# A 32-step V sum written as a register loop on TensorE, with the engine's program laid on a boundary

## The chip, the cores and the metric

The kernel runs on one NeuronCore of one Trainium2 chip. The core has five engines with an instruction stream each: TensorE (PE, matrix products; PEld is its weight loads), VectorE (DVE), ScalarE (ACT), GpSimd (POOL) and SyncE (SP), which here issues the large transfers. Sixteen DMA engines move data between HBM and the core's memories. The metric is the device time of one execution in microseconds, and the lower the better.

## The reference

One decode step of a transformer block: a single token `x` of 1024 values goes through a layernorm, and then through two branches in parallel, whose sum is added to `x`.

```python
q = (xn @ wq).reshape(1, 1, 32, 128)                 # 32 heads of 128
k, v = the last 4096 positions of 4 kv heads          # each serves 8 heads
o = softmax(q k^T / sqrt(128)) v                      # per head
a = o.reshape(1, 1, 4096) @ wo
h = gelu(layernorm(xn) @ w1 + b1)                     # 3584 hidden values
b = h @ w2 + b2
out = x + a + b      # x's own part enters with b2 in the first accumulation
```

All inputs are bf16. K, V and the four weight matrices are 39.85 MB in all, and each byte is read once.

## The kernel before, in words

**Slots and transfers.** The large operands go through a ring of four slots of 32 KB per partition (`slots`, line 64). Slot 0 holds k_sb, then w11, then wo0; slot 1 wq0, w10, w21; slot 2 wq1, v_sb, wo1; slot 3 the transposed K's scratch kt_scr, then w20. SP issues them in this order: K (four DMAs, line 74), wq0 and wq1 (line 91), w10 and w11 (line 203), V (three DMAs, line 209), w20 and w21 (line 217), wo0 in one DMA and wo1 in five (line 225), and the output last (line 354). A transfer into a slot waits, on SP, for the last reader of what the slot held. For wo1 that is the V sum, the matmuls that read v_sb. Every DMA adds to one of eight counters (semaphores) at its landing; the Tile framework hands them out in turn and writes all waits. K's fourth DMA counts on the eighth of them, and the next that counts there is w20.

**The attention.** K is transposed in blocks of 32 by VectorE (line 187), and the blocks are set in order by ScalarE and VectorE (lines 194 and 197) while TensorE makes q from wq (line 234). Scores for 4096 positions and 32 heads stand as four bands of 32 partitions with 1024 columns (line 272). Maximum, exponential (line 294) and a block transpose (line 296) give `eTb`, a tile of 128 partitions by 1024, in which columns 32c to 32c+31 are the 32 heads' weights for the 128 positions of chunk c. The V sum (lines 314 to 317) adds up over the 32 chunks c: weights `eTb[:, 32c:32c+32]`, moving data 512 columns of V (four kv heads of 128), result `o_all` of 32 heads by 512. A mask picks each head's own kv head, VectorE divides by the softmax sum and reduces (lines 319 to 323), and four small matmuls and a copy (lines 326 and 328) turn the result into `o8`, one column per step for Wo.

**The MLP.** w1's products (line 254) stand on TensorE between the steps of the softmax; gelu (line 309) and a transpose (line 311) give `hT`.

**The output.** w2 in 28 steps and Wo in 32 are taken as one list, `chunk_src`. All but the last eight steps add into `accf`, two halves of 512 columns (line 335); the last eight into `acct`, four quarters of 256 (line 350). When accf is done, four copies, by VectorE and ScalarE in turn, bring it into `bulk` (lines 345 and 347). VectorE adds acct and bulk into `res` (line 353), and SP writes it out. On TensorE the order is the one just told: V sum, o8, w20's steps, w21's, wo0's, wo1's. TensorE's stream is in order.

Of the kernel before, what the change touches and what calls it, by code (L numbers as in the profile page):

```python
# [8 lines left out]
FP32 = mybir.dt.float32  # L9
BF16 = mybir.dt.bfloat16  # L10
ACT = mybir.ActivationFunctionType
ALU = mybir.AluOpType
# [4 lines left out]
def kernel(  # L17
# [14 lines left out]
    nc = tc.nc  # L32
    P = 128
    D = A_x.shape[-1]
    Hkv = A_k_cache.shape[1]
    Sk = A_k_cache.shape[2]
    Dh = A_k_cache.shape[3]
    NQ = A_wq.shape[1]
    Hq = NQ // Dh
# [4 lines left out]
    NCH = W // P  # L44
    NJQ = NQ // 512
    WQ4 = W // 4
# [8 lines left out]
    consts = ctx.enter_context(tc.tile_pool(name="consts", bufs=1))  # L55
# [4 lines left out]
    ps_f = ctx.enter_context(tc.tile_pool(name="ps_f", bufs=2, space=bass.MemoryType.PSUM))  # L60
# [6 lines left out]
        return ring.tile([P, RING_ELEMS], BF16, tag=f"ring{slots[name]}", name=name, align_bytes=256)  # L67

    x_flat = A_x.rearrange("a b d -> (a b d)")


    k_sb = ring_tile("k_sb")
# [103 lines left out]
    for half in range(2):  # L176
        pr = 32 * half
        nc.tensor.matmul(accf[pr:pr + 1, :], lhsT=ones_bf[pr:pr + 2, 0:1], rhs=xb2[pr:pr + 2, :],
                         start=True, stop=False, tile_position=(pr, pr))
# [12 lines left out]
    for s in range(NS):  # L192
        for (R, Cd) in pairs[:ACT_PAIRS]:
            nc.scalar.copy(out=kT[32 * Cd:32 * Cd + 32, R, s, :].rearrange("p (c j) -> p c j", j=32),  # L194
                           in_=T5[32 * R:32 * R + 32, s, :, Cd, :])
    for (R, Cd) in pairs[ACT_PAIRS:]:
        nc.vector.tensor_copy(out=kT[32 * Cd:32 * Cd + 32, R, :, :].rearrange("p s (c j) -> p (s c) j", j=32),  # L197
                              in_=kt_scr[32 * R:32 * R + 32, :].rearrange("p (c a j) -> p c a j", a=4, j=32)[:, :, Cd, :])
# [7 lines left out]
    v4 = v_sb[:].rearrange("p (g c d) -> p g c d", g=Hkv, c=NCH)  # L206
# [22 lines left out]
    for i, w3 in enumerate(wq_tiles):  # L229
        for r in range(4):  # L230
            c = 4 * i + r
            for j in range(NJQ):
                b, t = divmod(j, 4)
                nc.tensor.matmul(accq[32 * t:32 * t + 1, b, :], lhsT=xnT[:, c:c + 1], rhs=w3[:, r, j * 512:(j + 1) * 512],  # L234
                                 start=(c == 0), stop=(c == C - 1), tile_position=(0, 32 * t))
# [8 lines left out]
    for j in range(8):  # L244
        t, b = divmod(j, 2)
        nc.tensor.matmul(acch[32 * t:32 * t + 1, b, :NH], lhsT=ones_bf[0:1, 0:1], rhs=b1_row[:, j * NH:(j + 1) * NH],
                         start=True, stop=False, tile_position=(0, 32 * t))
    for i, w3 in enumerate(w1_tiles):
        for r in range(4):
            c = 4 * i + r  # L250
            for b in range(2):
                for t in range(4):
                    j = 2 * t + b
                    nc.tensor.matmul(acch[32 * t:32 * t + 1, b, :NH], lhsT=yT[:, c:c + 1], rhs=w3[:, r, j * NH:(j + 1) * NH],  # L254
                                     start=False, stop=(c == C - 1), tile_position=(0, 32 * t))
# [11 lines left out]
    for a in range(WQ4 // 512):  # L267
        sp = ps_f.tile([P, 512], FP32, tag="pf", name="sp")
        for R in range(4):
            for g in range(Hkv):  # L270
                kv = kT[:, R, :, :].rearrange("p u (b r h) -> p h b u r", r=8, h=Hkv)[:, g, 16 * a:16 * a + 16]
                nc.tensor.matmul(sp[32 * R:32 * R + 32, :].rearrange("p (b r u) -> p b u r", r=8, u=4), lhsT=qm[:, g, :], rhs=kv,  # L272
                                 start=(g == 0), stop=(g == Hkv - 1), tile_position=(0, 32 * R))
# [18 lines left out]
    l_loc = small.tile([P, 1], FP32, tag="l_loc")  # L292
    e128 = consts.tile([P, WQ4], BF16)
    nc.scalar.activation(out=e128[:], in_=sc[:], func=ACT.Exp, bias=nmx[:], scale=scale, accum_out=l_loc[:])  # L294
    eTb = consts.tile([P, WQ4], BF16)
    nc.vector.transpose(out=eTb[:], in_=e128[:])
    rs_ps = ps_f.tile([Hq, 1], FP32, tag="pf", name="rs_ps")
    nc.tensor.matmul(rs_ps[:], lhsT=sel4[:], rhs=l_loc[:], start=True, stop=True)
    rs = small.tile([Hq, 1], FP32, tag="rs")
# [1 line left out]
    grs = small.tile([Hq, Hkv], FP32, tag="grs")  # L301
# [9 lines left out]
    nc.vector.transpose(out=hT[:], in_=h_sb[:].rearrange("p (d c) -> p c d", c=CW2))  # L311


    o_all = ps_f.tile([Hq, Hkv, Dh], FP32, tag="pf", name="o_all")
    for c in range(NCH):
        nc.tensor.matmul(o_all[:].rearrange("h g d -> h (g d)"), lhsT=eTb[:, 32 * c:32 * c + 32], rhs=v4[:, :, c, :],  # L316
                         start=(c == 0), stop=(c == NCH - 1))
    o_m = consts.tile([Hq, Hkv, Dh], FP32)
    nc.vector.tensor_tensor(out=o_m[:], in0=o_all[:], in1=grs[:].unsqueeze(2).to_broadcast([Hq, Hkv, Dh]), op=ALU.mult)  # L319
    o_f = consts.tile([Hq, Dh], FP32)  # L320
    nc.vector.tensor_reduce(out=o_f[:], in_=o_m[:].rearrange("h g d -> h d g"), axis=AX.X, op=ALU.add)
    o_bf = consts.tile([Hq, Dh], BF16)
# [10 lines left out]
    for idx, (kind, c, wap) in enumerate(chunk_src[:n_bulk]):  # L333
        for half in range(2):
            nc.tensor.matmul(accf[32 * half:32 * half + 1, :], lhsT=vec[kind](c), rhs=wap[:, half * 512:(half + 1) * 512],  # L335
                             start=False, stop=(idx == n_bulk - 1), tile_position=(0, 32 * half))
# [11 lines left out]
    for idx, (kind, c, wap) in enumerate(chunk_src[n_bulk:]):  # L348
        for t in range(4):
            nc.tensor.matmul(acct[32 * t:32 * t + 1, :], lhsT=vec[kind](c), rhs=wap[:, t * 256:(t + 1) * 256],  # L350
                             start=(idx == 0), stop=(idx == TAIL - 1), tile_position=(0, 32 * t))
# [33 lines left out]
```

## Time and profile before

Three runs took 102.22, 102.37 and 102.55 us; the median is 102.37. The profile is of one more execution, of which it gives the span (first to last instruction) and no wall time.

| | us |
|---|---|
| median of three runs | 102.37 |
| span of the profiled execution | 100.73 |
| median less span | 1.64 |
| TensorE matmuls busy | 46.8 (46% of the span) |
| VectorE busy | 45.6 (45%) |
| ScalarE busy | 32.1 (32%) |
| GpSimd busy | 4.5 (4%) |
| DMA, queue of the large transfers | 39.85 MB, 92.8% of 16 engines' span |
| V sum, line 316 | 32 matmuls, 7.1 busy, 379 ns mean of one |

The mean duration of a matmul is longer than its share of the time, since matmuls overlap in the array: 32 of 379 ns take 7.07 us from the first's start to the last's end. In the rows, a shape such as 128x512 is partitions by elements, and 128*32 before it is the part of the array that is used, rows by columns. "DMA x<-y" is a transfer, "SPq" is SP's issuing of it, and "[1.65 <-DMA v_sb...]" is the idle time ahead of a group and what ended it. The granted clock is TensorE's, 1.00 is full speed. Registers, branches and semaphore instructions are not counted as busy time of an engine.

### The profile page before, as it was taken

How to read it: one execution, taken by the hardware profiler on the slowest of the kernel's cores; microseconds unless marked ns; L12 is line 12 of the kernel's file. 1: busy time of each engine (PE TensorE's matmuls, PEld its weight loads, DVE VectorE, ACT ScalarE, POOL GpSimd, SP SyncE). 2: the span in 40 equal slices, each digit the busy share in tenths (PEclk: the TensorE clock that was granted, in tenths of full speed). 3: DMA queues.
4: the chain of work that ended last, by engine and by line, in shares of the span. 5: the costliest groups of instructions: out<-in, count | busy, mean ns of one | idle time of the engine just before them, and what ended most of it. 6: DMA issues, size and time to landing. Idle time of an engine off the chain costs nothing.

```text
span 100.7 us, 934 instructions
## 1 busy us (share of the span) xinstructions
PE 46.8 (46%) x361; PEld 18.6 (18%) x361; DVE 45.6 (45%) x63; ACT 32.1 (32%) x35; POOL 4.5 (4%) x18
## 2 busy tenths in 40 slices
PE   0250300007500940048956357991980980299830
PEld 0120200002100300024402233431320320033310
DVE  4650369999999999941215246009000000000220
ACT  0500000899999999940020453000000000000110
POOL 7160200000000000000000000000000000000000
PEclk9999999999995579555599999999578599958995
DMA  1999999999999899898999998998999999999910
GB/s 27 393 417 417 416 429 494 442 455 455 429 416 390 376 512 387 376 524 376 381 420 426 433 525 387 447 451 376 490 410 425 416 416 429 416 420 415 393 41 1
DMA packets 2646, 39.92 MB, mean 396 GB/s; under 512 B 457, under 2 KB 465, under 8 KB 850
## 3 DMA queue, kind: packets, MB, share of 16 engines
q1 hardware_dynamic: 2488, 39.85, 92.8%
q8 instruction: 3, 0.05, 0.2%
q10 hardware_dynamic: 154, 0.01, 0.1%
q14 instruction: 1, 0.01, 0.0%
HBM read 39.86 MB, written 0.00 MB: 396 GB/s over the span
## 4 chain that ended last, share of the span: by engine, by line
DMA 82%; PE 11%; SPq 2%; issue 1%; DVE 0%; DVEq 0%
DMA wo<-in_A_wo_dram 27%; DMA wq<-in_A_wq_dram 26%; DMA v_sb<-in_A_v_cache_dram 23%; PE o_all L316 7%; DMA k_sb<-in_A_k_cache_dram 5%; PE accq L234 4%; SPq L225 2%; SPq L209 1%; DVE res L353 0%; PE acct L350 0%; DVEq L353 0%
## 5 line engine op out<-in xcount | busy, mean ns | idle before, releaser
L194 ACT COPY kT<-kt_scr 32x1024 bf16<-32x1024 bf16 x24 | 25.0, 1042 | 13.8 <-DVE kt_scr L187 13.5
L187 DVE STREAM_TRANSPOSE kt_scr<-k_sb 128x4096 bf16<-128x4096 bf16 x4 | 17.4, 4413 | 1.0 <-DMA k_sb<-in_A_k_cache_dram 1.0
L234 PE MATMUL accq<-wq,xnT 128*1 128x512 bf16 x64 | 7.0, 618 | 18.3 <-DMA wq<-in_A_wq_dram 18.3
L197 DVE COPY kT<-kt_scr 32x4096 bf16<-32x4096 bf16 x10 | 12.2, 1219 | 0.2
L345 DVE COPY bulk<-accf 1x256 f32<-1x256 f32 x2 | 0.8, 416 | 24.6 <-PE accf L335 24.1
L347 ACT COPY bulk<-accf 1x256 f32<-1x256 f32 x2 | 0.7, 362 | 34.3 <-DVE bulk L345 34.3
L335 PE MATMUL accf<-w,hT 128*1 128x512 bf16 x56 | 9.5, 514 | 2.8 <-DMA w<-in_B_w_dram 2.8
L335 PE MATMUL accf<-wo,o 128*1 128x512 bf16 x48 | 7.0, 464 | 5.0 <-DMA wo<-in_A_wo_dram 5.0
L316 PE MATMUL o_all<-v_sb,eTb 128*32 128x512 bf16 x32 | 7.1, 379 | 1.6 <-DMA v_sb<-in_A_v_cache_dram 1.6
L234 PEld LDWEIGHTS <-xnT 128*1 128x1 bf16 x64 | 2.1, 116 | 22.4 <-issue 22.4
L272 PE MATMUL sp<-kT,qm 128*32 128x512 bf16 x32 | 6.0, 949 | 0.3 <-DVE qm L263 0.3
L258 PE MATMUL qT_ps<-ident,q_sb 128*128 128x128 bf16 x8 | 1.2, 308 | 7.7 <-DVE q_sb L237 7.7
L335 PEld LDWEIGHTS <-hT 128*1 128x1 bf16 x56 | 3.0, 106 | 8.8 <-issue 7.5
L335 PEld LDWEIGHTS <-o 128*1 128x1 bf16 x48 | 2.5, 98 | 9.5 <-issue 7.6
L316 PEld LDWEIGHTS <-eTb 128*32 128x32 bf16 x32 | 3.0, 97 | 5.6 <-issue 2.1
L254 PE MATMUL acch<-w,yT 128*1 128x448 bf16 x64 | 3.4, 352 | 0.0
L272 PEld LDWEIGHTS <-qm 128*32 128x32 bf16 x32 | 2.3, 165 | 3.3 <-issue 3.3
L319 DVE TENSOR_TENSOR o_m<-o_all,grs 32x512 f32<-32x512 f32 x1 | 0.7, 679 | 4.9 <-PE o_all L316 4.9
L277 ACT COPY sc<-sp 128x512 f32<-128x512 f32 x1 | 0.6, 587 | 7.1 <-PE sp L272 7.1
L311 DVE STREAM_TRANSPOSE hT<-h_sb 128x896 bf16<-128x896 bf16 x1 | 1.7, 1719 | 2.4 <-ACT h_sb L309 2.4
L275 DVE COPY sc<-sp 128x512 f32<-128x512 f32 x1 | 0.7, 692 | 3.8 <-PE sp L272 3.8
L294 ACT ACTIVATE e<-sc,nmx 128x1024 bf16<-128x1024 f32 x1 | 1.1, 1147 | 3.9 <-DVE nmx L291 3.9
(84 smaller groups left out, 34.3 us busy)
## 6 DMA issues: line engine op xcount, KB each, us to landing
w<-in_B_w_dram SPq DMA_DIRECT2D x4, 3584.0 KB, 22.2
wq<-in_A_wq_dram SPq DMA_DIRECT2D x2, 4096.0 KB, 23.1
k_sb<-in_A_k_cache_dram SPq DMA_DIRECT2D x4, 1024.0 KB, 7.4
wo<-in_A_wo_dram SPq DMA_DIRECT2D x1, 4096.0 KB, 28.2
v_sb<-in_A_v_cache_dram SPq DMA_DIRECT2D x1, 2048.0 KB
v_sb<-in_A_v_cache_dram SPq DMA_DIRECT2D x2, 1024.0 KB, 22.5
wo<-in_A_wo_dram SPq DMA_DIRECT2D x1, 2048.0 KB
wo<-in_A_wo_dram SPq DMA_DIRECT2D x1, 1024.0 KB
```

What stands on the lines that cost most here:

```text
L187: nc.vector.transpose(out=scr[:, s, :], in_=k2[:, s, :])
L194: nc.scalar.copy(out=kT[32 * Cd:32 * Cd + 32, R, s, :].rearrange("p (c j) -> p c j", j=32), in_=T5[32 * R:32 * R + 32, s, :, Cd, :])
L197: nc.vector.tensor_copy(out=kT[32 * Cd:32 * Cd + 32, R, :, :].rearrange("p s (c j) -> p (s c) j", j=32), in_=kt_scr[32 * R:32 * R + 32, :] ...
L225: nc.sync.dma_start(out=tv[:, a:b, :], in_=wo_v[:, nr * i + a:nr * i + b, :])
L234: nc.tensor.matmul(accq[32 * t:32 * t + 1, b, :], lhsT=xnT[:, c:c + 1], rhs=w3[:, r, j * 512:(j + 1) * 512], start=(c == 0), stop=(c == C ...
L254: nc.tensor.matmul(acch[32 * t:32 * t + 1, b, :NH], lhsT=yT[:, c:c + 1], rhs=w3[:, r, j * NH:(j + 1) * NH], start=False, stop=(c == C - 1) ...
L258: nc.tensor.transpose(qT_ps[:, b * 4 + hh, :], q_sb[:, b, hh * Dh:(hh + 1) * Dh], ident[:])
L272: nc.tensor.matmul(sp[32 * R:32 * R + 32, :].rearrange("p (b r u) -> p b u r", r=8, u=4), lhsT=qm[:, g, :], rhs=kv, start=(g == 0), stop=( ...
L294: nc.scalar.activation(out=e128[:], in_=sc[:], func=ACT.Exp, bias=nmx[:], scale=scale, accum_out=l_loc[:])
L311: nc.vector.transpose(out=hT[:], in_=h_sb[:].rearrange("p (d c) -> p c d", c=CW2))
L316: nc.tensor.matmul(o_all[:].rearrange("h g d -> h (g d)"), lhsT=eTb[:, 32 * c:32 * c + 32], rhs=v4[:, :, c, :], start=(c == 0), stop=(c == ...
L335: nc.tensor.matmul(accf[32 * half:32 * half + 1, :], lhsT=vec[kind](c), rhs=wap[:, half * 512:(half + 1) * 512], start=False, stop=(idx == ...
```

## The change

Three things change.

- At the start of the body, `nc.tensor.addr_align(256, 0, 0)` makes the loader put TensorE's next instruction on a multiple of 256 instructions; TensorE branches over the padding.
- `eTb` gets 96 more columns, set to zero by GpSimd, and each step of the V sum takes 128 weight columns instead of 32: those of chunk c and of the three chunks behind it. The result tile `o_win` has 128 rows, of which the first 32 are the V sum as before, and the others are not read.
- Of the 32 steps, the first two and the last two stand alone, and the 28 between are a loop of 14 rounds on TensorE with two steps in a round. The addresses of weights and moving data come from registers. A round has, besides two weight loads and two matmuls, three packed register instructions (of six, two and six operations), two single ones and a compare-and-branch.

The whole stands in a critical section. In the built program, every engine's stream is cut there by a branch. TensorE's branch into the section waits for all eight DMA counters, and for the counters of VectorE, ScalarE, GpSimd and of itself, at the values reached by the instructions recorded ahead of the section; the eighth DMA counter is waited for at the value that w20's landing gives it. Before, the first weight load and matmul of the V sum waited for v_sb's three DMAs and for eTb. Behind the section TensorE has a semaphore instruction, a drain and a no-op, the last of which releases VectorE's line 319 (328 after) and SP's first DMA of wo1. On the other engines the order of the work is as before.

```diff
+    nc.tensor.addr_align(256, 0, 0)
...
-    eTb = consts.tile([P, WQ4], BF16)
-    nc.vector.transpose(out=eTb[:], in_=e128[:])
+    eTb = consts.tile([P, WQ4 + 96], BF16)
+    nc.gpsimd.memset(eTb[:, WQ4:], 0.0)
+    nc.vector.transpose(out=eTb[:, :WQ4], in_=e128[:])
...
-    o_all = ps_f.tile([Hq, Hkv, Dh], FP32, tag="pf", name="o_all")
-    for c in range(NCH):
-        nc.tensor.matmul(o_all[:].rearrange("h g d -> h (g d)"), lhsT=eTb[:, 32 * c:32 * c + 32], rhs=v4[:, :, c, :],
-                         start=(c == 0), stop=(c == NCH - 1))
+    o_win = ps_f.tile([P, Hkv, Dh], FP32, tag="pf", name="o_win")
+    o_all = o_win[0:Hq]
+    o_flat = o_win[:].rearrange("h g d -> h (g d)")
+    with tc.tile_critical():
+        for c in range(2):
+            nc.tensor.matmul(o_flat, lhsT=eTb[:, 32 * c:32 * c + P], rhs=v4[:, :, c, :], start=(c == 0), stop=False)
+        with nc.tensor.Fori(1, NCH // 2 - 1, 1) as i:
+            for u in range(2):
+                nc.tensor.matmul(o_flat, lhsT=eTb[:, bass.ds(64 * i + 32 * u, P)], rhs=v4[:, :, 2 * i + u, :], start=False, stop=False)
+        for c in range(NCH - 2, NCH):
+            nc.tensor.matmul(o_flat, lhsT=eTb[:, 32 * c:32 * c + P], rhs=v4[:, :, c, :], start=False, stop=(c == NCH - 1))
     o_m = consts.tile([Hq, Hkv, Dh], FP32)
-    nc.vector.tensor_tensor(out=o_m[:], in0=o_all[:], in1=grs[:].unsqueeze(2).to_broadcast([Hq, Hkv, Dh]), op=ALU.mult)
+    nc.vector.tensor_tensor(out=o_m[:], in0=o_all, in1=grs[:].unsqueeze(2).to_broadcast([Hq, Hkv, Dh]), op=ALU.mult)
```

## The prediction

> **What bounds the kernel now.** I read the chain that ended last first, then TensorE's rows of the timeline, the waits, and the granted clock by stretch. The chain, from the V cache's transfer on (start, length, what):
>
> ```profile
> 37.41 23.43 DMA v_sb<-in_A_v_cache_dram
> 60.83 0.14 issue
> 60.97 7.08 PE o_all L316 x32
> 68.05 0.02 issue
> 68.06 0.33 SPq L225
> ...
> 69.86 27.49 DMA wo<-in_A_wo_dram
> 97.35 0.04 issue
> 97.39 0.31 PE acct L350 x4
> ...
> 97.79 0.42 DVE res L353
> ```
>
> It puts the V sum on the path, because wo1 goes into the slot that v_sb leaves. But most of those 27.49 us is queueing behind transfers that SP issued earlier. In the timeline TensorE starts on w21 at 77.95, on wo0 at 87.61, on wo1's last piece at 97.39, each as it lands:
>
> ```profile
> 60.97 7.07 PE L316 MATMUL o_all<-v_sb,eTb 128*32 128x512 bf16 x32 [1.65 <-DMA v_sb<-in_A_v_cache_dram]
> ...
> 70.27 4.87 PE L335 MATMUL accf<-w,hT 128*1 128x512 bf16 x28
> ...
> 77.95 4.66 PE L335 MATMUL accf<-w,hT 128*1 128x512 bf16 x28 [2.81 <-DMA w<-in_B_w_dram]
> ...
> 87.61 7.03 PE L335 MATMUL accf<-wo,o 128*1 128x512 bf16 x48 [5.00 <-DMA wo<-in_A_wo_dram]
> ```
>
> v_sb to w21 is 7.34 MB in 17.1 us (429 GB/s), wo0 to wo1's end 4.19 MB in 9.74 us (430 GB/s): one even stream. That stream of 39.85 MB is the bound, wo1 must only be issued before it runs dry at 87.6, and it is issued at 68. The reader also sees TensorE's slack behind the V sum: 2.81 and 5.00 us of waits.
>
> The clock of those bursts (stretch, busy times, granted clock, DMA share, GB/s):
>
> ```profile
> 72.00:74.00 2.00, 2.00 (x12) 0.61 (x10) 0.00 (x0) 0.00 (x0) 0.00 (x0) 0.50 0.96 416
> 77.90:80.00 2.10, 2.05 (x10) 0.62 (x11) 0.00 (x0) 0.00 (x0) 0.00 (x0) 0.50 1.12 484
> 91.20:94.65 3.45, 3.44 (x32) 1.25 (x28) 0.00 (x0) 0.00 (x0) 0.00 (x0) 1.00 0.99 412
> ```
>
> Each burst after an idle stretch runs its first 3.0 to 3.8 us at half clock (70.3 to 74.1, 78.0 to 81.0, 87.6 to 91.2). A pair of these matmuls takes 0.427 us there (weight loads at 71.09, 71.51, 71.94) and 0.215 at full clock (32 in 3.44 us). The V sum ran at full clock, 7.07 / 32 = 0.221 us each.
>
> **The change, part by part.** The profiled execution has a span of 100.73 us and no wall time of its own; the median of the three runs, 102.37, stands 1.64 above it, and I add that to every span.
>
> *The boundary.* TensorE jumps over the padding once at its start. Price: from zero to one fetch of code, for which the nearest row is x_sb's 1.7 us from issue to landing. TensorE's first matmul waits for VectorE until 3.60, and after the second it waits for the xb transfer until 9.98. I take zero on the path; if that cover went, the layernorm would be late next, and VectorE's K transposes have 0.97 us in hand there.
>
> *The memset of 128x96 on GpSimd.* ident's, 128x128, takes 0.19 us. It stands behind rstd's first power, where GpSimd then idles 3.98 us for ve: zero; without that cover it would delay rstd2. The two extra block branches of SP, VectorE and ScalarE stand where those queues wait several us: zero.
>
> *The wait ahead of the section.* This is the part to look for. Before, the V sum waits for v_sb's three transfers and eTb. Now TensorE's branch into the section waits for every counter at the value reached by what was recorded ahead of it, and the eighth DMA counter, which counted K's fourth transfer, next counts w20. So the V sum waits for w20, which it doesn't read. w20 and w21 are equal, so w20 lands halfway between 60.83 and 77.95: 69.4. All else is earlier (hT ends at 63.2, acch's matmuls at 59.3). With two sequencer steps the section starts at 69.6 instead of 60.97. Behind that wait on TensorE: o8, all of w2, all of Wo; SP waits with wo1, VectorE with o_m.
>
> *The loop's pace.* No loop runs in this trace. TensorE's sequencer does, per pair, three packed register instructions (6, 2 and 6 operations), two single ones, a compare-and-branch, and two weight loads and two matmuls whose addresses come from registers. The rows near it:
>
> ```profile
> L316 PEldq EVENT_SEMAPHORE  x1: 51/51/51, 60.9 to 60.9; - x1
> ...
> L114 POOLq MOVE  x1: 29/29/29, 5.9 to 5.9; - x1
> ```
>
> The one instruction that TensorE's sequencer handles alone takes 51 ns, and the weight load behind it starts 80 ns after it did (60.86 to 60.94). An extra operation in a packed instruction lies between 11 ns (SP's semaphore instruction takes 17 ns with one condition, 28 with two) and GpSimd's register move, 29. A weight load or matmul costs at least 26 ns of issue (64 in 1.69 us at L254), at most another 80.
> Lowest: 6 x 51 + 4 x 26 = 0.41 us, hidden below the pair's 0.44. Middle-low: 6 x 80 + 11 x 11 + 4 x 26 = 0.70. High: 6 x 80 + 11 x 29 + 4 x 80 = 1.12. I take 0.90, half way between the last two, because the start-to-start 80 ns is nearer to what a stream of such steps costs than the bare 51.
> [...]
> At 0.90 the loop is bound by the sequencer at either clock (0.854 cold): first two matmuls issued in 0.27, 14 x 0.90 = 12.6, the last two 0.7; together 13.6 instead of 7.08. The V sum ends at 69.6 + 13.6 = 83.2 instead of 68.05.
> 128 weight columns instead of 32: three of spread's 128-column loads take 0.14 us, so a load stays behind a matmul of 0.22; zero. The 96 extra result rows cost nothing in a stream set by 512 columns; at most the 8 ns per matmul above 0.213 go, 0.26 us in all.
>
> *What follows the V sum.* Three sequencer steps to release o_m (0.25), then as now 2.22 to the first w2 matmul (68.05 to 70.27). Then nothing waits: w20, w21 and (from 87.6) wo0 have landed. 104 matmuls are 52 pairs: 3.6 us at half clock do 8.4, the other 43.6 take 9.4, together 13.0. Then the four bulk copies, 94.65 to 96.4 now, 1.8 to res. Sum 17.3, so res starts at 83.2 + 17.3 = 100.5 instead of 97.79. The tail's 32 acct matmuls (0.038 each) run beside the copies. wo1 is issued at 83.5, four us before the stream runs dry, so it lands as now.
>
> The sum: 2.7 us later, span 103.4, time **105.1**. The point from which it shows: the V sum must end by 97.79 - 17.3 = 80.5, so a pair may cost 0.71 (10.9 = 0.27 + 14 x 0.71 + 0.7). At 0.41 the array sets the pace, 8.4 matmuls in 3.6 us cold and 23.6 x 0.221: the V sum ends at 78.4 and nothing is lost. At 1.12 it ends at 86.3: +5.8, 108.2.
>
> **The rivals.**
> *The slack holds (same).* If register steps run ahead of the array at under 0.71 us a pair, the V sum ends by 80.5 and the end is again the stream: 102.4. For it: 2.81 and 5.00 us of waits to eat, and the lower bounds above. Against: it needs ten instructions at under 70 ns each.
> *The chain taken at its word.* If wo1's landing followed its issue by 27.5 us, the end would move by 83.2 - 68.05: 117.5. Against it: the even 430 GB/s.
> *Each back edge fetches code.* At x_sb's 1.7 us a fetch, 13 taken back edges add 22 us: about 127. For it: the change itself says that it places code on a boundary of 256. Against it: counted from the boundary the loop stands at about 399 to 409, inside one stretch of 256. [...]
> *Faster.* In 82.5 to 87.5 the stream moved 377 GB/s, below its 430: 0.27 MB, 0.6 us. wo1's pieces are then queued with wo0's; issued later they could leave wo0 alone, and the time would be 101.8. It decides only where the V sum ends by 80.5. Against it: TensorE idles in that stretch, and 70 to 75 with the same queue has 436.
>
> **How the numbers follow.** A measurement of this kernel tells about 0.3% from no change (runs 102.22 to 102.55). Slower by the loop's pace 0.76, by fetches 0.03, by the chain 0.01; slack holds 0.14; faster 0.06. The likeliest is 105.1, its own range 102.8 to 108.6. The range of 8 in 10 leaves out the faster case and the top of the slow ones (loop at over 1.15, fetches, chain): 102.0 to 108.6.
>
> **What would show it.** TensorE's first matmul of the V sum at 69.5 to 69.8, released by w20; pairs 0.8 to 1.0 us apart; last at about 83; no wait for w21, and at most a short one for wo0; accf's last matmul at 98 to 99 instead of 94.6, res behind bulk's copies; wo1's end still at about 97.4. Pairs under 0.7 apart with a wait for wo0 left would make it wrong, and so would gaps of microseconds between pairs, or a V sum that starts at 61.

## The result, and the profile after

The changed kernel took 104.42 us as the median of four runs (103.22 to 105.01), the kernel before 102.39 beside it (102.22 to 102.55). The ratio is 1.0153, with a 95% interval of 1.0116 to 1.0190: slower by 1.2 to 1.9%. The forecast was 105.1, range 102.0 to 108.6. The profiled execution has a span of 103.3 us and took 105.01, the longest of the four; the ratio leaves it out (the other three have a median of 104.21), and two later traces, at 104.68 and 104.71, show the same course.

The chain that ended last, of the changed kernel, from the V sum's end on (start, length, what):

```profile
83.23 0.69 DVE o_m L328
83.95 1.02 DVE o_f L330
...
85.26 0.25 PE o_ps L335 x4
85.50 12.47 PE accf L344 x99
...
98.55 0.42 DVE bulk L354
...
99.05 0.37 ACT bulk L356
...
99.45 0.43 DVE bulk L354
...
99.90 0.37 ACT bulk L356
...
100.29 0.42 DVE res L362
```

Before, this chain ended with a transfer: wo1's last piece at 97.35, four matmuls, res at 97.79. Now there is no transfer in it at all behind the V sum. TensorE runs from 85.26 to the end of accf without a wait, the four copies into bulk follow, and res starts at 100.29, 2.5 us later.

TensorE's rows of the timeline:

```profile
69.99 1.03 PE L321 MATMUL o_win<-v_sb,eTb 128*128 128x512 bf16 x2 [11.42 <-DMA w<-in_B_w_dram]
70.82 5.50 PE L324 MATMUL o_win<-v_sb,eTb 128*128 x14
76.55 0.67 PE L324 MATMUL o_win<-v_sb,eTb 128*128 x2 [0.24 <-issue]
77.46 0.63 PE L324 MATMUL o_win<-v_sb,eTb 128*128 x2 [0.24 <-issue]
...
82.39 0.60 PE L326 MATMUL o_win<-v_sb,eTb 128*128 128x512 bf16 x2
85.26 0.25 PE L335 MATMUL o_ps<-o_bf,spread 32*128 32x32 bf16 x4 [2.26 <-DVE o_bf L332]
85.43 7.89 PE L344 MATMUL accf<-w,hT 128*1 128x512 bf16 x56
93.16 4.92 PE L344 MATMUL accf<-wo,o 128*1 128x512 bf16 x44
```

The V sum's first matmul now starts at 69.99, and what ended the wait ahead of it is a transfer of w2, which the V sum doesn't read. From 76 on, every round of two matmuls has a gap of 0.24 us behind it in which TensorE waits for nothing but its own sequencer. The waits of 2.81 us for w21 and 5.00 us for wo0, which stood between the bursts on w2 and Wo, are gone: 56 and 44 matmuls stand back to back.

The loop's instructions on TensorE's sequencer (engine, instruction, count, shortest/median/longest in ns), of the changed kernel:

```profile
L322 PEldq FUSED_REGOPS  x14: 78/78/83, 70.1 to 81.6; - x14
L322 PEldq ALU_OP  x14: 32/32/32, 70.6 to 82.2; - x14
L322 PEldq COMPARE_BRANCH  x14: 76/208/223, 70.7 to 82.3; - x14
...
L324 PEldq FUSED_REGOPS  x28: 42/58/79, 70.2 to 81.9; - x28
```

The branch back is the dearest of them: a median of 208 ns where it is taken, 76 the one time it is not. In the records of a round at full clock, the first step takes 0.26 and 0.30 us in turn from its first register instruction to the next step's, the second 0.25, and the counter and the branch 0.36 to the next round's first instruction. So rounds start 0.864 and 0.904 us apart in turn, 0.884 in the mean.

### The profile page after: what moved, and what is told of

Its sections match the earlier page's. It is cut to its first block, busy times and chain, and to the rows that moved or that the text cites. A ratio compares the mean times of both kernels' runs of the same rounds, so it can differ in the third digit from the quotient of the medians.

```text
span 103.3 us, 1033 instructions
## 1 busy us (share of the span) xinstructions
PE 45.7 (44%) x361; PEld 17.7 (17%) x361; DVE 45.8 (44%) x63; ACT 32.1 (31%) x35; POOL 4.6 (4%) x19
## 5 line engine op out<-in xcount | busy, mean ns | idle before, releaser
L324 PE MATMUL o_win<-v_sb,eTb 128*128 x28 | 10.0, 477 | 1.7 <-issue 1.7
L328 DVE TENSOR_TENSOR o_m<-o_win,grs 32x512 f32<-32x512 f32 x1 | 0.7, 679 | 20.8 <-PEq L319 20.8
L344 PE MATMUL accf<-w,hT 128*1 128x512 bf16 x56 | 7.9, 452 | 0.0
L321 PE MATMUL o_win<-v_sb,eTb 128*128 128x512 bf16 x2 | 1.0, 618 | 11.4 <-DMA w<-in_B_w_dram 11.4
L344 PE MATMUL accf<-wo,o 128*1 128x512 bf16 x48 | 5.3, 379 | 0.0
L273 PE MATMUL sp<-kT,qm 128*32 128x512 bf16 x32 | 4.8, 763 | 0.3 <-DVE qm L264 0.3
L324 PEld LDWEIGHTS o_win<-v_sb,eTb 128*128 x28 | 3.1, 112 | 9.0 <-issue 8.4
L133 PE MATMUL ln_tot<-st,ones_f 128*128 128x1 f32 x2 | 0.6, 362 | 4.8 <-DVE st L131 4.8
```

Of the source, the lines that this page charges most:

```text
L324: nc.tensor.matmul(o_flat, lhsT=eTb[:, bass.ds(64 * i + 32 * u, P)], rhs=v4[:, :, 2 * i + u, :], start=False, stop=False)
L328: nc.vector.tensor_tensor(out=o_m[:], in0=o_all, in1=grs[:].unsqueeze(2).to_broadcast([Hq, Hkv, Dh]), op=ALU.mult)
```

## The experiments

My theory was that two things are needed at once: the start, held up by the section's wait for w20, and the loop's pace. Together they put the V sum's end past about 80.5, from where TensorE's work behind it no longer fits ahead of the last transfer. The main rivals were that one of the two alone does it (the chain of waits of before has the V sum on it), and that boundary or weight width count.

### The section without the loop

```diff
-        with nc.tensor.Fori(1, NCH // 2 - 1, 1) as i:
-            for u in range(2):
-                nc.tensor.matmul(o_flat, lhsT=eTb[:, bass.ds(64 * i + 32 * u, P)], rhs=v4[:, :, 2 * i + u, :], start=False, stop=False)
+        for c in range(2, NCH - 2):
+            nc.tensor.matmul(o_flat, lhsT=eTb[:, 32 * c:32 * c + P], rhs=v4[:, :, c, :], start=False, stop=False)
```

> The section and its wait for w20 stay, the register loop is written out (32 matmuls with fixed addresses, 128 weight columns). Theory (late start and slow pace are both needed to use up TensorE's slack): V sum from about 70.0, half clock at first, last result at 78.5 to 79.5, before the point 80.5; res waits for the stream again, 102.2 to 102.7. Rival 'the late start alone delays wo1 and with it the end': the V sum ends some 11 us later than before, so 110 or more. Rival 'the section itself costs': above 103 although the V sum ends by 79.5.

Measured: 102.61 us, ratio 1.0007 (0.9983 to 1.0031). TensorE's rows in this run:

```profile
70.00 1.04 PE L321 MATMUL o_win<-v_sb,eTb 128*128 128x512 bf16 x2 [11.04 <-DMA w<-in_B_w_dram]
70.82 7.26 PE L323 MATMUL o_win<-v_sb,eTb 128*128 128x512 bf16 x28
...
80.95 6.21 PE L343 MATMUL accf<-w,hT 128*1 128x512 bf16 x56
87.90 3.62 PE L343 MATMUL accf<-wo,o 128*1 128x512 bf16 x32 [0.74 <-DMA wo<-in_A_wo_dram]
92.75 1.89 PE L343 MATMUL accf<-wo,o 128*1 128x512 bf16 x16 [1.23 <-DMA wo<-in_A_wo_dram]
```

The V sum starts as late as in the changed kernel and ends at 78.5, 10.5 us later than before, and nothing is lost: TensorE waits for wo0 and wo1 again, and res starts at 98.06. wo1's last transfer, issued 10.6 us later (80.48 instead of 69.86), lands 0.26 us later (97.61 instead of 97.35). So the V sum's place on the chain of before was no bound. That chain named the last thing that wo1's issue waited for, not what wo1's landing waited for.

### The loop without the wait for w20

The transfers of w2 and Wo are recorded behind the section, with an edge that keeps them there, so that SP issues them behind its branch. SP doesn't wait there; order, slots and waits of the transfers stay. TensorE's wait on the eighth counter then is the one for K's fourth transfer.

```diff
-    with tc.tile_critical():
+    with tc.tile_critical() as section:
+        marker = section.name
...
+        dma = nc.sync.dma_start(out=tv, in_=w2_v[:, nr * i:nr * (i + 1), :])
+        tc.add_manual_dep(dma.ins, marker, mybir.DependencyInfo(mybir.DependencyClass.NoSync, mybir.DependencyReason.DATA))
...
```

> The loop stays as in the changed kernel; w2's and Wo's transfers are placed behind the section's branch in SP's stream (same order, same slots, no new wait), so that TensorE's branch into the section waits for v_sb and hT but not for w20. Theory: V sum from 62.5 to 63.5, pairs 0.88 apart, last result at 75 to 76.5, before 80.5, so nothing is lost: 102.2 to 102.7. Rival 'the loop's pace alone costs': 13.0 instead of 7.1 us on the chain, 5 to 8 us more than before.

Measured: 102.70 us, ratio 1.0008 (0.9984 to 1.0031). TensorE's rows:

```profile
63.56 1.03 PE L304 MATMUL o_win<-v_sb,eTb 128*128 128x512 bf16 x2 [4.37 <-DVE hT L295]
...
75.43 0.67 PE L307 MATMUL o_win<-v_sb,eTb 128*128 x2 [0.24 <-issue]
75.97 0.60 PE L309 MATMUL o_win<-v_sb,eTb 128*128 128x512 bf16 x2
...
87.59 6.84 PE L346 MATMUL accf<-wo,o 128*1 128x512 bf16 x48 [2.38 <-DMA wo<-in_A_wo_dram]
```

The same loop at the same pace, 13.0 us from first matmul to last result, from 63.56 to 76.57, costs nothing. With the run before it, this shows that neither half of the change's cost exists alone.

### One step a round, and four

The third and fourth runs change the pace alone. With one step, the loop has 28 rounds; with four it has 6, and eight steps are written out.

```diff
-        with nc.tensor.Fori(1, NCH // 2 - 1, 1) as i:
-            for u in range(2):
-                nc.tensor.matmul(o_flat, lhsT=eTb[:, bass.ds(64 * i + 32 * u, P)], rhs=v4[:, :, 2 * i + u, :], start=False, stop=False)
+        with nc.tensor.Fori(2, NCH - 2, 1) as i:
+            nc.tensor.matmul(o_flat, lhsT=eTb[:, bass.ds(32 * i, P)], rhs=v4[:, :, i, :], start=False, stop=False)
```

> 28 rounds of one step instead of 14 of two: one more counter step and one more compare-and-branch for every two steps, nothing else. From the changed kernel's trace a round is 0.30 for the step and 0.36 for the counter and the branch, 0.66 in all; 28 x 0.66 = 18.5, V sum's last result at 88.5 to 89.5 instead of 83.0. Theory (TensorE bounds the end, one for one): 5.5 to 6.5 us above the changed kernel, 109 to 111. Here wo1 is issued after the stream has run dry at 87.6, so a gap of about 3 us in the DMA row, without effect on the end. Rival 'the end was set by wo1's landing': the end moves by the gap only, about 105 to 106.

Measured: 111.26 us (110.45 to 111.64), ratio 1.0863 (1.0815 to 1.0912). The V sum's last result is at 88.45, 5.5 us later than in the changed kernel, and res starts at 105.74, 5.45 later; the profiled execution took 110.45, and the median lies a little above what was expected. Two lines of the chain, then stretches of time (the last three columns are granted clock, DMA share and GB/s):

```profile
90.95 12.47 PE accf L343 x99
...
105.74 0.42 DVE res L361
```

```profile
80.00:87.60 7.60, 7.21 (x14) 1.51 (x14) 0.00 (x0) 0.00 (x0) 0.00 (x0) 0.50 0.68 293
87.60:92.00 4.40, 2.14 (x17) 0.72 (x16) 2.36 (x5) 0.00 (x0) 0.00 (x0) 0.89 0.56 186
92.00:96.00 4.00, 4.00 (x26) 1.30 (x22) 0.00 (x0) 0.00 (x0) 0.00 (x0) 0.62 1.00 422
```

The stream does run dry here, because wo1 is issued only when the V sum is done. Its gap shows in the 293 and 186 GB/s, against 422 behind it. The end still follows TensorE, one for one, and not the gap: wo1's last piece lands at 101.96, 3.8 us before res starts.

The other, four steps a round:

```diff
-        with nc.tensor.Fori(1, NCH // 2 - 1, 1) as i:
-            for u in range(2):
-                nc.tensor.matmul(o_flat, lhsT=eTb[:, bass.ds(64 * i + 32 * u, P)], rhs=v4[:, :, 2 * i + u, :], start=False, stop=False)
+        for c in range(2, 4):
+            nc.tensor.matmul(o_flat, lhsT=eTb[:, 32 * c:32 * c + P], rhs=v4[:, :, c, :], start=False, stop=False)
+        with nc.tensor.Fori(1, 7, 1) as i:
+            for u in range(4):
+                nc.tensor.matmul(o_flat, lhsT=eTb[:, bass.ds(128 * i + 32 * u, P)], rhs=v4[:, :, 4 * i + u, :], start=False, stop=False)
+        for c in range(28, 30):
+            nc.tensor.matmul(o_flat, lhsT=eTb[:, 32 * c:32 * c + P], rhs=v4[:, :, c, :], start=False, stop=False)
```

> Six rounds of four steps, eight steps written out: a round is 0.30 + 3 x 0.25 + 0.36 = 1.40 for four steps. Theory: V sum's last result at 81 to 82, about 1.5 us earlier than in the changed kernel, and the time follows: 102.7 to 103.5. Rival 'the slack does not end at 80.5': 102.4 or as slow as the changed kernel, 104.4.

Measured: 102.56 us, ratio 0.9992 (0.9972 to 1.0012). The V sum's last result is at 79.3, not at 81 to 82. Of the eight steps that are written out, the four ahead of the loop cost next to nothing: the loop's first register instruction stands at 70.03, 0.11 us behind the first matmul, while the array still has those four to do. The four behind it ran at 0.22 us each; the granted clock had risen at 72.6 in this run. The end is before 80.5, and nothing is lost:

```profile
81.75 7.89 PE L348 MATMUL accf<-w,hT 128*1 128x512 bf16 x56
89.47 5.35 PE L348 MATMUL accf<-wo,o 128*1 128x512 bf16 x48
95.14 0.61 PE L363 MATMUL acct<-wo,o 128*1 128x256 bf16 x16 [0.31 <-DMA wo<-in_A_wo_dram]
```

TensorE doesn't wait any more on w2 and on the steps that add into accf. What waiting is left stands between the last eight steps of Wo, 0.31 us here and 0.65, 0.20 and 0.36 behind it. This is close to the point where the slack ends: V sum ends of 76.6, 78.5 and 79.3 cost nothing, 83.0 starts res 2.5 us later than before, 88.45 starts it 7.95 later.

### Without the boundary, with narrow weights, and both without section and loop

```diff
-    nc.tensor.addr_align(256, 0, 0)
```

> The changed kernel without the line that lays TensorE's program on a boundary of 256; the loop then stands wherever the loader puts it. Theory (the boundary is worth nothing here, a short loop is not fetched again): 103.2 to 105.0 as the changed kernel, rounds 0.88 us apart. Rival 'the boundary keeps the loop from a fetch per round': rounds more than 1.5 us apart and 10 us or more on the time.

Measured: 104.75 us (104.68 to 105.71), ratio 1.0249 (1.0214 to 1.0283). Rounds are as in the changed kernel (gaps of 0.24 and 0.28 us behind the pairs), the V sum ends at 82.7, res starts at 99.99, and the branch takes a median of 208 ns. No round has a longer gap. The ratio is above the changed kernel's 1.0153 (1.0116 to 1.0190), and no row of the trace explains that. The five executions have spans of 102.8 to 103.0, against 101.5 to 103.3 for the changed kernel, and what makes the two longest (105.71 and 105.46) longer lies outside the span. So the boundary is worth nothing in the rounds; below 1 us the times don't tell. Where the loader put the loop in this run the trace doesn't tell, so whether the place of a loop can count is left open.

```diff
-    o_win = ps_f.tile([P, Hkv, Dh], FP32, tag="pf", name="o_win")
+    o_win = ps_f.tile([Hq, Hkv, Dh], FP32, tag="pf", name="o_win")
...
-                nc.tensor.matmul(o_flat, lhsT=eTb[:, bass.ds(64 * i + 32 * u, P)], rhs=v4[:, :, 2 * i + u, :], start=False, stop=False)
+                nc.tensor.matmul(o_flat, lhsT=eTb[:, bass.ds(64 * i + 32 * u, Hq)], rhs=v4[:, :, 2 * i + u, :], start=False, stop=False)
...
```

> The changed kernel with 32 weight columns in every step and 32 result rows, as before the change; boundary, section and loop stay. Theory (weight loads lie behind the matmuls and the sequencer sets the pace): rounds 0.88 us apart, 103.2 to 105.0. Rival 'the wide weights carry part of the pace': rounds shorter or longer by over 0.03, and the time with them by 0.4 or more.

Measured: 104.72 us (104.33 to 104.80), ratio 1.0207 (1.0189 to 1.0225): rounds 0.88 apart, V sum from 69.70 to 82.70, res at 99.99. Here the width of the weights has no part in the pace: 0.88 us a round with 32 columns, 0.884 with 128.

```diff
+    nc.tensor.addr_align(256, 0, 0)
...
+    o_win = ps_f.tile([P, Hkv, Dh], FP32, tag="pf", name="o_win")
+    o_all = o_win[0:Hq]
     for c in range(NCH):
-        nc.tensor.matmul(o_all[:].rearrange("h g d -> h (g d)"), lhsT=eTb[:, 32 * c:32 * c + 32], rhs=v4[:, :, c, :],
+        nc.tensor.matmul(o_win[:].rearrange("h g d -> h (g d)"), lhsT=eTb[:, 32 * c:32 * c + P], rhs=v4[:, :, c, :],
```

> The kernel before with the boundary and the 128 weight columns, but no section and no loop: the V sum written out in the ordinary stream. Theory: V sum from 61.0 to 68.1 at 0.22 a matmul, time as before, 102.2 to 102.7. Rival 'wide weights shorten the V sum': under 0.215 a matmul; it would still not show in the time.

Measured: 102.48 us, ratio 0.9995 (0.9982 to 1.0009). The row of the V sum is the one of before with other weights:

```profile
61.14 7.07 PE L319 MATMUL o_win<-v_sb,eTb 128*128 128x512 bf16 x32 [1.97 <-DMA v_sb<-in_A_v_cache_dram]
```

7.07 us for 32 matmuls of 128 weight columns, as with 32 columns. The memset of eTb's 96 columns is in this kernel too. All of the loss comes from the section and its loop.

### An early start with a slow pace

The last run joins two edits, the transfers behind the section and one step a round.

> Both edits at once: the section does not wait for w20 (V sum from about 63.6), and the loop takes one step a round. The loop took 18.5 us from the first matmul to the last result in the run with one step a round; so the V sum ends at 82.1, and res starts 17.3 later, at 99.4 instead of 97.8. Theory (only the sum of start and pace counts, from 80.5 on): 1.6 us above before, 103.9; 102.9 where the w2 burst happens to run at full clock. Rival 'without the wait for w20 nothing is lost': 102.2 to 102.7. Rival 'one step a round costs its 6 us again': above 106.

Measured: four executions of 104.24, 105.02 (the profiled one), 106.94 and 107.08 us, with the kernel before at 102.50 beside them. The first two are 1.7 and 2.5 us above it, where 1.6 was expected, and lie between the two rivals. The other two are above 106, at a mean granted clock of 0.773 against 0.901 in the profiled one; they left no trace, and what made them longer stays open. In the profiled one the theory's side held and its size did not. The V sum ends at 81.89, as expected (82.1), but res starts at 100.33 instead of 99.4:

```profile
63.33 1.03 PE L304 MATMUL o_win<-v_sb,eTb 128*128 128x512 bf16 x2 [4.37 <-DVE hT L295]
...
73.04 7.99 PE L306 MATMUL o_win<-v_sb,eTb 128*128 x13 [0.23 <-issue]
80.83 1.06 PE L308 MATMUL o_win<-v_sb,eTb 128*128 128x512 bf16 x2
84.15 0.26 PE L336 MATMUL o_ps<-o_bf,spread 32*128 32x32 bf16 x4 [2.26 <-DVE o_bf L333]
84.34 9.03 PE L345 MATMUL accf<-w,hT 128*1 128x512 bf16 x56
```

The w2 burst takes 9.03 us here, against 7.89 in the changed kernel. The granted clock was at half from 73.0 to 90.1: it fell while the thin loop ran, and the burst behind it had 5.7 us at half speed instead of the 3.6 that I reckon with. So the price of this slow loop isn't only its own length: the next burst began at half clock, and took 1.1 us longer than in the changed kernel.

## Why the prediction was right

By its own steps, against the changed kernel's trace:

- *The wait ahead of the section.* Forecast: V sum from 69.6, released by w20. It started at 69.99, and the row names the transfer of w2. TensorE's last semaphore instruction ahead of the section, the one with the eighth DMA counter, starts at 69.66, right behind w20's landing at 69.63. The entry took 0.33 us from there to the first weight load, of which the branch is 0.17, and not the 0.16 of two sequencer steps. The run without that wait shows that it is this wait which costs.
- *The loop's pace.* 0.90 forecast, 0.884 measured; the terms were off both ways, and that they made up for each other is luck. Counter and branch back take 0.36 of it, where I had two steps of 0.08; the single register instructions are 32 to 42 ns and the packed ones 42 to 83. From the start of one of them to the next 0.09 to 0.16 us pass, and that has the weight loads and matmuls in it, for which I had 0.10 to 0.32 a round on their own. The compare-and-branch alone takes a median of 208 ns taken and 76 not taken, and 0.27 us pass from a taken one's start to the next instruction's.
- *The V sum's end.* 83.2 forecast, 82.99 measured (82.39 + 0.60).
- *What follows.* Forecast 17.3 us from there to res: 0.25 to o_m, 2.22 to the first w2 matmul, 13.0 for 104 matmuls, 1.8 to res. Measured: 0.24, 2.20, 13.1 (85.43 to 98.50) and 1.79, in all 17.3. Of the burst on w2, 3.4 us were at half clock (85.7 to 89.1), where I had 3.6.
- *The slack.* The point 80.5 lies between 79.3, which cost nothing, and 83.0.
- *Boundary, memset, weight width:* priced at zero; the kernel with the three alone takes as long as the one before (ratio 0.9995), and the rounds are the same without the boundary and with narrow weights.

What was off is the total: 2.7 us more was forecast, the ratio gives 1.6 (1.2 to 1.9). The profiled execution took 105.01, but the shortest run of the four took 103.22, with a mean granted clock of 0.945 where the others had 0.830 to 0.845. The term is the half-clock start of the burst on w2. I had taken it as certain, because all three bursts of the trace of before began so. It isn't: the burst took 6.21 us where the clock stayed full behind the V sum (the first two experiments), 7.89 where it fell. Two stretches, from the changed kernel and from the run without the loop (the last three columns are again granted clock, DMA share and GB/s):

```profile
85.50:89.00 3.50, 3.50 (x19) 1.05 (x20) 0.22 (x2) 0.00 (x0) 0.00 (x0) 0.53 0.99 405
...
80.90:87.20 6.30, 6.26 (x60) 2.47 (x58) 0.34 (x2) 0.00 (x0) 0.00 (x0) 1.00 0.96 410
```

That 1.7 us is about the spread between 103.22 and 105.01. That the short run owes its time to it is argued, since it left no trace, but its clock speaks for it. The traces of the kernel before and of the changed one show a clock of 0.50 or 1.00 and nothing between. By that, a mean of 0.945 over a span of 101.5 us leaves 11.2 us at half clock (2 x 0.055 x 101.5), an estimate. The half-clock stretch that begins in the wait for w20 lasts 10.2 or 13.7 us in each trace with that wait, so a further 3.4 us on w2 find no room. What decides whether the clock falls there, no run tests. The stretches of one clock inside the span last 3.41, 6.83, 10.24 and 20.48 us in the trace of before, 3.41, 10.24, 13.65 and 17.07 in that of the changed kernel, so 3.41 or a whole multiple of it; the half clock of the last run, 73.0 to 90.1, is five times 3.41. Counted in such steps, in the changed kernel one of them (82.3 to 85.7) holds all of the 2.3 us for which TensorE idles behind the V sum, and half clock follows. In the run without the loop the same 2.3 us fall on two, which meet at 79.8, and the clock stays full. Whether that is the cause these two cases don't show. So it is partly luck that the profiled execution came within 0.1 us of the forecast.

Of the rivals, the slack that holds is what the run without the loop and the one with four steps a round show. The chain taken at its word fell with the first experiment, the fetch at every back edge with the 0.27 us from a taken branch to the next instruction, where that rival had 1.7. My argument against it, that the loop lies inside one stretch of 256, no run tests. The faster case, wo1 issued later leaving wo0 alone, has nothing for it: wo0 landed between 87.5 and 87.9 in every trace, even where it had the queue alone (one step a round, 87.67), and wo1's last piece no earlier than before, at 97.3 to 98.3 wherever the stream stayed full.

## What to carry to other kernels

A critical section of Tile waited here, with a loop in it and without one (the V sum started at 69.99 and 70.00; in the first of these w20 landed at 69.63), on the engine that enters it, for everything recorded or scheduled ahead of it, transfers for later stages too; look at what each counter of that wait counts before pricing the section's inside. Where a chain of waits ends in a long transfer, compare its landing with the stream's rate: here wo1, issued 10.6 us later while the stream stayed full, landed 0.26 us later. And of an engine that waits for transfers, add up its work behind the moved step: the point at which the sum no longer fits is where a change begins to cost, here 12.4 us after the V sum's old end of 68.05.

## What the runs showed that I had not expected

- This register loop on TensorE costs 0.36 us a round for its counter and branch, and 0.25 to 0.30 for each step's registers, weight load and matmul. At four steps a round the sequencer is at 0.35 a step (two rounds start 1.39 us apart, at 75.90 and 77.29), still slower than the array's 0.22 at full clock.
- The clock fell in the thinner loop. With two matmuls in 0.88 us, about half of the time at 0.22 each, the clock stayed at 1.00 from 75.4 to the loop's end at 82.4; with one in 0.61, about a third, it fell back to half after 3.4 us (78.0 in the run with one step a round) and after 6.8 us (73.0 in the last run). No run has a load between the two. The rows of the run with one step a round, before and after the fall:

```profile
76.00:78.00 2.00, 1.27 (x4) 0.31 (x4) 0.00 (x0) 0.00 (x0) 0.00 (x0) 1.00 0.98 424
78.40:86.00 7.60, 7.19 (x13) 1.36 (x13) 0.00 (x0) 0.00 (x0) 0.00 (x0) 0.50 0.90 388
```
- This loop's own pace hardly feels the clock: a round is 0.88 at full clock, where the sequencer sets it (gaps of 0.24 us with nothing but the sequencer to wait for), and a pair at half clock takes 0.85.
